# VectorE's half of the closing copy waits for TensorE only: a decode step on one NeuronCore

## The chip, the cores and the metric

The kernel runs on one core of one Trainium2 chip. The metric is the device time of one execution in microseconds (us); lower is better. The core has TensorE (PE in the profile), VectorE (DVE), ScalarE (ACT), GpSimd (POOL) and SyncE (SP), each with its own instruction stream, and 16 DMA engines. TensorE writes its results to PSUM, a small memory of 128 partitions by 8 banks (the kernel calls the whole of it `banks`); VectorE and ScalarE read PSUM and write SBUF, the main on-chip memory; DMAs move data between SBUF and HBM. The engines run side by side, and one waits for another through semaphores.

## The reference, cut to what matters

One token (batch 1, sequence 1, width 512) goes through an attention block over a cache of 16384 keys and values (32 query heads, 8 key heads of width 128), and then through a mixer with an MLP. All inputs are bfloat16.

```python
h  = x + attention(layernorm(x), k_cache, v_cache, wq, wo)
# block B, for one position:
#   its shift by one or two positions leaves only padding (zeros) when S is 1,
#   so x1 = x and w1, w2 do not count
x1 = layernorm(h)
h2 = gelu(layernorm(x1) @ w3) @ w4          # 512 -> 1792 -> 512
out = h + (x1 + h2)                          # 512 numbers
```

The result is one row of 512 bfloat16 numbers, 1 KB. The reading is 79 MB: 67 MB of keys and values and the weights `wq`, `wo`, `w3` and `w4`.

## The kernel before, in words

The keys and values come in pairs of heads, four pairs (`PAIRS`), the keys of a pair in two pieces of 4 MB; `load` puts these DMAs, and those of the weights, on SP's queue. For each pair the kernel transposes the keys on VectorE (line 583), multiplies them by the query on TensorE (line 600), takes the softmax (lines 610 to 625), multiplies by the values (line 636) and gathers the heads (lines 652 to 660). After the last pair come the product with `wo` (line 702), the second normalisation (`row_sums(1, ...)` and `variance(1)`), the product with `w3` (line 720), the gelu on ScalarE in two halves (line 729) with a transpose on VectorE behind each (line 733), and the product with `w4` (lines 737 to 751).

That last product is written to a piece of one PSUM bank, `n_ps`, in 14 steps `m`, one for each slice of `w4`. In each step four small matmuls write four groups of 32 partitions, one for each block of 128 columns of the result; every partition of a group holds the same numbers. In the middle four more matmuls (line 740) add `xsum`, which holds h plus x1. So after the last matmul the 512 numbers stand in `n_ps` as four blocks of 128 columns, on partitions 0 to 31, 32 to 63, 64 to 95 and 96 to 127.

Two copies take them out, changing float32 to bfloat16. ScalarE's (line 752) reads partitions 0 to 63 of `n_ps` into columns 0 to 127 of `fin`, an SBUF tile of 64 partitions by 256 columns. VectorE's (line 754) reads partitions 64 to 127 of the same columns of `n_ps` into columns 128 to 255 of `fin`, on the same 64 partitions. Then one DMA from SP's queue (line 755) takes rows 31 and 32 of `fin` to the output in HBM, and SP waits for its landing (line 757).

No planner sets the order: every engine runs its list of operations in the order of the program, and `Program.op` works out what each has to wait for. An operation names the tiles that it reads (`r`), those that it writes (`w`), and the PSUM banks that it touches (`bank`). It waits for the last writer of what it reads, for the writer and the readers of what it writes, and, for each bank that it names, for the last operation of every other engine that named that bank, whether that one read or wrote:

```python
for k in bank:
    for e, o in self.users.get(k, {}).items():
        if e != eng:
            need(o, False)
```

The bank of `n_ps` has the key "mn". Both copies name it, as do the matmuls of lines 740 and 747. `_wants` then turns the operations waited for into one semaphore value for each engine, and `_run` issues a wait for each value that the engine has not seen yet, ahead of the operation (line 137). A wait that doesn't fit into the operation itself stands in the trace as an instruction of its own with line 137.

On VectorE and on TensorE, `dve(None)` and `pe(None)` mark a place where a branch that is never taken is put (lines 150 and 314); VectorE's stands ahead of the copy of line 754, which is VectorE's last operation.

Of the kernel before, what the change touches and what calls it, by code (L numbers as in the profile page):

```python
# [342 lines left out]
def bass_sequential_preLN__gqa_block_cached__mixer_s_mlp__decode_kernel(  # L343
# [13 lines left out]
    with ExitStack() as ctx:  # L357
# [58 lines left out]
        fin = sb("fin", [64, 256], BF16)  # L416
# [13 lines left out]
        m_ps, n_ps = mn_ps[:, 0:256], mn_ps[:, 256:512]  # L430
# [28 lines left out]
        def dve(fn, r=(), w=(), bank=()):  # L459
            return P.op("DVE", fn, r, w, bank)  # L460
# [11 lines left out]
        def piece(cuts, m):  # L472
            return [lo <= m < hi for lo, hi in cuts].index(True)
# [23 lines left out]
        def variance(i):  # L497
# [30 lines left out]
            r=["ident", "x4"], w=["quarter"])  # L528
# [9 lines left out]
            r=["ident_f"], w=["row32"])  # L538
        dve(lambda e: e.tensor_reduce(maskdd[:, :], ident_f[:, :].rearrange("p (n d) -> p d n", d=4), AX.X, ALU.add),
            r=["ident_f"], w=["maskdd"])  # L540
# [6 lines left out]
        for z, m, key, mk in ((zo, rowgh, "zo", "rowgh"), (zd, maskgh, "zd", "maskgh")):  # L547
# [5 lines left out]
            r=["hT", (("st", 0), 0), (("st", 0), 6)] + [("v", x) for x in range(VP)], w=["xn"])  # L553
# [3 lines left out]
        for i, key in enumerate(keys):  # L557
            P.part("query", i)
            for k in range(NCH):
                pe(lambda e, k=k: e.matmul(row[:, bass.ds(P.b, 512)], copies(xn[:, k:k + 1], 128),  # L560
                                           wq_k[:, k, bass.ds(P.c, REP * DH)], start=(k == 0), stop=(k == NCH - 1)),
                   r=["xn"], also=[("v", x) for x in range(VP)], w=["n" if key == "mn" else key], bank=[key])
        P.part()
        for g in range(2):
            half = banks[64 * g:64 * g + 64, PAIRS * g:PAIRS * g + PAIRS, :].rearrange("p j c -> p (j c)")
            for b in range(2):
# [3 lines left out]
                    r=["n" if x == "mn" else x for x in keys[PAIRS * g:PAIRS * g + PAIRS]], w=["qcol"],  # L570
                    bank=keys[PAIRS * g:PAIRS * g + PAIRS])
# [120 lines left out]
        for n, (lo, hi) in enumerate(W4):  # L692
# [4 lines left out]
            r=["o_m"], w=["o_f"])  # L697
        dve(lambda e: e.tensor_copy(o_b[:, :], o_f[:, :]), r=["o_f", ("r", 0, 0)], w=["o_b"])

        for r_ in range(32):  # L700
# [3 lines left out]
               r=["o_b"] + [("r", 0, n) for n in (piece(WO, r_),) if n], w=[("O", 0)], bank=[("O", 0)])  # L704
        h_ps, hkey = banks[:, 6, :], "spare0"
        dve(lambda e: e.tensor_copy(osum[:, :], O_ps[0][:, :]), r=[("O", 0)], w=["osum"], bank=[("O", 0)])
        for q in range(4):
            pe(lambda e, q=q: e.matmul(h_ps[32 * q:32 * q + 32, 0:128], copies(row32[:, 0:1], 32),
                                       osum[:, q * 128:(q + 1) * 128], start=True, stop=True),
               r=["osum", "row32"], w=[hkey], bank=[hkey])  # L710
# [4 lines left out]
            r=["hT", (S, 0)] + [("r", 1, 0)], w=["hc"])  # L715


        for k in range(NCH):
            for q in range(4):
                pe(lambda e, k=k, q=q: e.matmul(s_ps[32 * q:32 * q + 32, 0, 0:FQ], hc[:, k, :],  # L720
                                                w3_sb[:, k, q * FQ:(q + 1) * FQ], start=(k == 0), stop=(k == NCH - 1)),
                   r=["hc"] + [("r", 1, n) for n in (piece(W3, k),) if n], w=[("s", 0)], bank=[("s", 0)])
# [3 lines left out]
            r=["hr", "xs", (S, 6)], w=["xsum"])  # L726
# [10 lines left out]
        for m in range(NHC):  # L737
            if m == NHC // 2:
                for o in range(4):
# [3 lines left out]
                       r=["ident_f", "xsum"], w=["n"], bank=["mn"])  # L743
            if m == W4[-2][0]:
                pe(None)
            for o in range(4):
# [4 lines left out]
                   r=[("hcol", 2 * m // NHC), ("r", 1, len(W3) + piece(W4, m))], w=["n"], bank=["mn"])  # L751
        act(lambda e: e.activation(fin[:, 0:128], n_ps[0:64, 0:128], ACTF.Identity),  # L752
            r=["n"], w=[("fin", 0)], bank=["mn"])
        dve(lambda e: e.tensor_copy(fin[:, 128:256], n_ps[64:128, 0:128]), r=["n"], w=[("fin", 1)], bank=["mn"])  # L754
        P.op("SP", lambda e: e.dma_start(out[0, 0:1, :].rearrange("o (q j) -> (o q) j", q=2), fin[31:33, :]),
             r=[("fin", 0), ("fin", 1)], w=["out"], dma="out")
        P.op("SP", lambda e: e.nop(), r=["out"])
# [31 lines left out]
```

## Time and profile before

| what | value |
|---|---|
| time, median of 3 runs | 190.62 us (190.58, 190.62, 190.89) |
| the profiled execution's own time | 191.29 us |
| its span, from the first to the last instruction | 189.7 us |
| mean granted TensorE clock | 0.823 |
| PE, DVE, ACT, POOL busy | 116.1, 115.4, 9.3, 5.7 us |
| read from HBM | 79.17 MB, 417 GB/s over the span |
| ScalarE's copy, line 752 | 270 ns, once |
| VectorE's copy, line 754 | 293 ns, once |

Times in the views count from the first instruction. A row of the timeline gives the start, the length, the engine, the line, the operation, and then "out<-in" with the tiles' names; in square brackets stands how long the engine was idle before it, and what ended that. The chain of waits is the work that ended last, followed back from the end: each piece has its start and length, and "issue" is time in which nothing that the profile shows was waited for. An engine's name with a q (SPq, DVEq) means its sequencer: waits and DMA issues, which are not counted as busy. The ends of matmuls are modelled.

### The profile page before, as it was taken

What the parts mean: (1) busy time and instruction counts of PE and PEld (TensorE: products, weight loads), DVE (VectorE), ACT (ScalarE), POOL (GpSimd) and SP (SyncE); (2) the same over time, 40 slices, a digit from 0 to 9 for tenths busy, and PEclk for the clock granted to TensorE, in tenths of its full rate; (3) what the DMA queues carried; (4) which work ended last, traced back from release to release, by engine and by line L of the source; (5) the groups of instructions that cost most, each with busy time, mean ns of one, the idle gap of its engine ahead of it and who ended that gap; (6) DMA issues with size and microseconds to landing.
All of it is one profiled execution on the core that took longest, in us unless ns stands there. A gap on an engine that the chain in (4) does not pass through costs nothing.

```text
span 189.7 us, 2177 instructions
## 1 busy us (share of the span) xinstructions
PE 116.1 (61%) x701; PEld 45.8 (24%) x701; DVE 115.4 (61%) x140; ACT 9.3 (5%) x16; POOL 5.7 (3%) x10
## 2 busy tenths in 40 slices
PE   1009709997194498950842999606539996094544
PEld 1004203442031143320310343202213432041113
DVE  4900799995514998945047989460469896604151
ACT  3000000000200000002000000020000000500020
POOL 1900000000000000000000000000000000000010
PEclk9999985999858589995597599975975999759955
DMA  6999999999899999997999998999999999999992
GB/s 221 442 435 442 442 442 449 442 442 442 380 435 408 435 553 428 442 442 339 435 428 422 477 401 387 442 442 435 442 442 442 428 428 415 422 402 416 411 411 106
DMA packets 3613, 79.19 MB, mean 417 GB/s; under 512 B 410, under 2 KB 540, under 8 KB 1564
## 3 DMA queue, kind: packets, MB, share of 16 engines
q1 hardware_dynamic: 3604, 79.17, 97.5%
q8 instruction: 1, 0.02, 0.0%
q10 hardware_dynamic: 8, 0.00, 0.0%
HBM read 79.17 MB, written 0.00 MB: 417 GB/s over the span
## 4 chain that ended last, share of the span: by engine, by line
DMA 66%; DVE 15%; PE 14%; issue 3%; SPq 1%; ACT 0%; DVEq 0%
DMA kb<-in_A_k_cache_dram 46%; DMA kb<-in_B_w_dram 14%; DVE kt L583 13%; PE banks L600 8%; DMA vb<-in_A_wq_dram 7%; PE banks L560 4%; SPq L434 1%; DVE qcol L567 1%; PE banks L594 1%; PE banks L747 1%; DVE qb L574 0%; PE banks L740 0%; DVE xn L551 0%; DVE fin L754 0%; ACT fin L752 0%
## 5 line engine op out<-in xcount | busy, mean ns | idle before, releaser
L583 DVE STREAM_TRANSPOSE kt<-kb 128x2048 int32<-128x2048 int32 (+1 forms) x37 | 71.3, 1988 | 5.8 <-DMA kb<-in_A_k_cache_dram 4.2
L600 PE MATMUL banks<-kt,qn 128*128 x256 | 69.8, 422 | 0.2
L600 PEld LDWEIGHTS banks<-kt,qn 128*128 x256 | 26.6, 104 | 41.9 <-issue 25.1
L636 PE MATMUL banks<-vb,pt 128*32 128x512 bf16 x256 | 22.8, 534 | 2.8 <-POOLq L449 2.8
L652 DVE TENSOR_SCALAR od<-banks,rowc 128x128 f32<-128x128 f32 x4 | 1.4, 351 | 24.7 <-PE banks L636 24.7
L594 PE MATMUL banks<-qn 128*128 128x512 bf16 x8 | 3.9, 494 | 18.4 <-DVE kt L583 18.4
L560 PE MATMUL banks<-vb,xn 128*128 x32 | 8.4, 428 | 10.1 <-DVE xn L551 10.1
L625 DVE STREAM_TRANSPOSE pt<-p_sb 64x1024 bf16<-64x1024 bf16 x8 | 9.9, 1239 | 5.4 <-ACT p_sb L621 5.3
L636 PEld LDWEIGHTS banks<-vb,pt 128*32 128x32 bf16 x256 | 8.6, 130 | 15.2 <-issue 10.3
L621 ACT ACTIVATE p_sb<-banks,bias 128x1024 bf16<-128x1024 f32 x4 | 4.5, 1114 | 155.8 <-DVE nmh L617 155.8
L643 PE MATMUL banks<-acc,zd 128*32 128x1 f32 x8 | 1.1, 203 | 17.7 <-DVE pt L625 17.7
L610 DVE TENSOR_REDUCE mx<-banks 128x1 f32<-128x1024 f32 x4 | 4.9, 1224 | 8.1 <-PE banks L600 8.1
L567 DVE STREAM_TRANSPOSE qcol<-banks 64x1024 f32<-64x1024 f32 x4 | 4.8, 1226 | 6.4 <-PE banks L560 6.4
L560 PEld LDWEIGHTS banks<-vb,xn 128*128 128x128 bf16 x32 | 3.5, 108 | 14.6 <-issue 11.8
L509 POOL TENSOR_TENSOR st<-st,expo 128x1 f32<-128x1 f32 (+1 forms) x2 | 1.3, 630 | 176.1 <-DVE st L507 176.1
L613 PE MATMUL banks<-mxd,mean 128*128 128x128 f32 x8 | 2.0, 326 | 6.6 <-DVE mxd L611 6.6
L594 PEld LDWEIGHTS banks<-qn 128*128 128x128 bf16 x8 | 0.8, 100 | 20.8 <-issue 20.5
L658 PE MATMUL banks<-od,zo 128*32 128x128 f32 x8 | 1.6, 284 | 6.5 <-DVE od L655 6.5
L643 PEld LDWEIGHTS banks<-acc,zd 128*32 128x32 f32 x8 | 0.7, 140 | 18.4 <-DVE pt L625 18.4
L655 DVE SCALAR_TENSOR_TENSOR od<-banks,rowc,od 128x128 f32<-128x128 f32 x12 | 4.2, 351 | 0.4
L702 PE MATMUL banks<-kb,o_b 128*32 128x512 bf16 x32 | 2.7, 384 | 2.4 <-DMA kb<-in_A_wo_dram 1.3
L548 DVE COPY zo<-rowgh 128x32 f32<-128x32 f32 x1 | 3.6, 3627 | 0.0
(71 smaller groups left out, 42.4 us busy)
## 6 DMA issues: line engine op xcount, KB each, us to landing
kb<-in_A_k_cache_dram SPq DMA_DIRECT2D x8, 4096.0 KB, 29.7
vb<-in_A_v_cache_dram SPq DMA_DIRECT2D x2, 4096.0 KB, 29.6
vb<-in_A_wq_dram SPq DMA_DIRECT2D x1, 4096.0 KB, 12.6
kb<-in_A_wo_dram SPq DMA_DIRECT2D x2, 1536.0 KB, 25.4
kb<-in_B_w_dram SPq DMA_DIRECT2D x2, 640.0 KB, 25.4
kb<-in_B_w_dram SPq DMA_DIRECT2D x1, 896.0 KB, 22.4
kb<-in_B_w_dram SPq DMA_DIRECT2D x2, 448.0 KB, 23.4
kb<-in_A_wo_dram SPq DMA_DIRECT2D x1, 768.0 KB, 28.5
```

What stands on the lines that cost most here:

```text
L548: dve(lambda e, z=z, m=m: e.tensor_copy(z[:, :].rearrange("p (n d) -> p n d", d=4), m[:, :, :].rearrange("p g h -> p (g h)").unsqueeze(2). ...
L560: pe(lambda e, k=k: e.matmul(row[:, bass.ds(P.b, 512)], copies(xn[:, k:k + 1], 128), wq_k[:, k, bass.ds(P.c, REP * DH)], start=(k == 0), s ...
L567: dve(lambda e, g=g, b=b, half=half: e.transpose(qcol[64 * g:64 * g + 64, 2 * b:2 * b + 2, :, :].rearrange("p e m u -> p (e m u)"), half.r ...
L583: P.op("DVE", lambda e, view=view: e.transpose(view(kt), view(kb[y])), r=[("r", y, i) for i in range(RPARTS)], w=[("kt", t + i) for i in r ...
L594: pe(lambda e: e.matmul(row[:, bass.ds(P.y, 512)], copies(none, 128), copies(none, 512), start=True, stop=False, skip_group_check=True), r ...
L600: pe(lambda e, n=n: e.matmul(row[:, bass.ds(P.y, 512)], qn[:, n, bass.ds(P.q, 128)], key_piece(P.k, n), start=False, stop=(n == 3), skip_g ...
L610: dve(lambda e: e.tensor_reduce(mx[:, :], s_all, AX.X, ALU.max), r=[("s", 0), ("s", 1)], w=["mx"], **both)
L621: act(lambda e: e.activation(p_sb[:, :], s_all, ACTF.Exp, bias=bias[:, 0:1], scale=float(SCALE), accum_out=acc[:, :]), r=[("s", 0), ("s", ...
L625: dve(lambda e, g=g: e.transpose(pt[64 * g:64 * g + 64, :, :, g, :], p_sb[64 * g:64 * g + 64, :]), r=["p"], w=["pt"])
L636: pe(lambda e, l=l, ct=ct, ch=ch: e.matmul(O_ps[0][32 * ct:32 * ct + 32, :], pt[:, l, ch, :, :].rearrange("p g u -> p (g u)"), tiles[:, l ...
L655: dve(lambda e, block=block, c=c: e.scalar_tensor_tensor(od[:, :], block, rowc[:, c:c + 1], od[:, :], ALU.mult, ALU.add), r=[key, "rowc", ...
L702: pe(lambda e, r_=r_, q=q: e.matmul(O_ps[0][32 * q:32 * q + 32, :], copies(o_b[:, r_:r_ + 1], 32), wo_sb[:, r_ * D:(r_ + 1) * D], start=(r ...
```

## The change

VectorE's copy of the second half no longer names the bank "mn". It still reads "n", which the last matmul wrote, so it still waits for TensorE. The wait for ScalarE's copy, which came only from the bank, is gone. ScalarE's copy and the closing DMA with its two inputs, `("fin", 0)` and `("fin", 1)`, are as before. No later operation names the bank.

```diff
         act(lambda e: e.activation(fin[:, 0:128], n_ps[0:64, 0:128], ACTF.Identity),
             r=["n"], w=[("fin", 0)], bank=["mn"])
-        dve(lambda e: e.tensor_copy(fin[:, 128:256], n_ps[64:128, 0:128]), r=["n"], w=[("fin", 1)], bank=["mn"])
+        dve(lambda e: e.tensor_copy(fin[:, 128:256], n_ps[64:128, 0:128]), r=["n"], w=[("fin", 1)])
         P.op("SP", lambda e: e.dma_start(out[0, 0:1, :].rearrange("o (q j) -> (o q) j", q=2), fin[31:33, :]),
              r=[("fin", 0), ("fin", 1)], w=["out"], dma="out")
```

## The prediction

> **What bounds the kernel now.** I read the page first, then the end of the chain of waits, then the timeline of the last microseconds, SP's waits, and last the DMA of that window.
>
> The page says what the run as a whole is made of:
>
> ```profile
> span 189.7 us, 2177 instructions
> PE 116.1 (61%) x701; PEld 45.8 (24%) x701; DVE 115.4 (61%) x140; ACT 9.3 (5%) x16; POOL 5.7 (3%) x10
> ...
> DMA  6999999999899999997999998999999999999992
> ...
> DMA 66%; DVE 15%; PE 14%; issue 3%; SPq 1%; ACT 0%; DVEq 0%
> ```
>
> The reader should see that the 16 DMA engines are busy in nine tenths of nearly every slice and that no engine passes 61%. The kernel is bound by its loads nearly all the way, and no edit on VectorE could shorten that stretch. But the last slice of the DMA row is a 2: at the very end the loads are over and the work hangs on the engines. The edit lies there, so the question belongs to the last slice alone. The chain of waits in the window from 187.5 us on:
>
> ```profile
> 187.42 0.34 PE banks L747 x10
> 187.76 0.02 issue
> 187.78 0.28 ACT fin L752
> 188.06 0.03 issue
> 188.09 0.02 DVEq L137
> 188.11 0.04 issue
> 188.16 0.29 DVE fin L754
> ```
>
> The last matmuls end at 187.76. ScalarE starts 0.02 us later and ends at 188.06. Only then does VectorE's wait (the row DVEq L137) go through, and its copy runs from 188.16 to 188.45. The two copies stand one behind the other, both on the chain. The timeline of the same stretch shows the same two copies, and what comes behind them:
>
> ```profile
> 187.78 0.27 ACT L752 ACTIVATE fin<-banks 64x128 bf16<-64x128 f32 x1 [3.04 <-PE banks L747]
> 188.16 0.29 DVE L754 CAST fin<-banks 64x128 bf16<-64x128 f32 x1 [2.69 <-ACT fin L752]
> 188.52 0.33 SPq L755 DMA_DIRECT2D out_dram<-fin  x1
> ```
>
> VectorE had been idle for 2.69 us when its copy began, and the profile names ScalarE's copy as what ended that. SP's waits name what the closing DMA waited for:
>
> ```profile
> SPq L137 <- DVE fin L754: 18.8, 1, 18.8
> SPq L757 <- DMA out_dram<-fin: 0.8, 1, 0.8
> ```
>
> So SP waited for VectorE's copy last, issued the output's DMA 0.07 us after it ended (188.45 to 188.52), spent 0.33 us on the issue, and waited 0.8 us more for the landing, up to the end of the span at 189.7. Nothing else goes on then. From 187.76 on, whatever ends the later of the two copies sooner ends the run sooner by as much.
>
> **The change part by part.** It removes one dependency of one instruction; nothing is moved and nothing is added.
>
> *The wait that goes.* VectorE's copy then starts when TensorE's last matmul is done. What that costs after a matmul is shown by ScalarE's row: 0.02 us of issue from 187.76 to 187.78. For VectorE itself the nearest place is its first transpose of `qcol`, which also waited for the end of matmuls:
>
> ```profile
> 14.15 8.38 PE banks L560 x32
> 22.53 0.02 issue
> 22.56 0.04 DVE qcol L567
> ```
>
> Here too it is 0.02 us of issue. I take 187.78 as the new start of VectorE's copy, the same as ScalarE's. The old start is 188.16, so the copy begins 0.38 us sooner. Put together from the chain, that is ScalarE's 0.28, then 0.03 of issue, 0.02 for the wait's own instruction, and 0.04 before the copy: 0.37, and 0.01 of rounding.
>
> *The copy itself.* It took 0.29 us alone and would now run beside ScalarE's, in the same PSUM bank but on other partitions, and both write into the same 64 partitions of `fin`. No row of the trace before has these two engines in one bank together. The bounds: the low end is nothing. The high end is that the one goes behind the other, ScalarE's whole 0.27 us. The nearest row is VectorE's pair of transposes of `hg`; the first ran while ScalarE was still writing the second half of the same tile:
>
> ```profile
> L733 DVE STREAM_TRANSPOSE hcol<-hg x2: 549/566/582, 184.4 to 184.9; 128x224 bf16<-128x224 bf16 x2
> L729 ACT ACTIVATE hg<-banks,st x2: 485/486/487, 183.9 to 184.3; 128x224 bf16<-128x224 f32 x2
> ```
>
> One of the two took 549 ns and the other 582, a difference of 0.03 us at the most that sharing can have cost there, and ScalarE's two agree within 2 ns. I take nothing for the sum, as the row that it is nearest to allows 0.03 at most, and keep 0.03 and 0.27 for the range. A gain from sharing is excluded: two copies do not shorten each other.
>
> [...]
>
> *What is late next.* VectorE's copy would end at 187.78 + 0.29 = 188.07 or 188.08; ScalarE's ends at 188.06. The two are level within 0.02 us, and the DMA waits for both. So ScalarE's copy is the next in line, and no more than 188.45 - 188.06 = 0.39 us can be had from this edit at all.
>
> *What follows.* The gap of 0.07 to the issue, the 0.33 and the 0.8 stay as they are; the DMA's issue moves from 188.52 to 188.14. The output's 1 KB has no other transfer to compete with or to be given way to, as the last loads are over: the DMA's rows for 187.3 to 188.3 list one packet, for instructions, and no data.
>
> ```profile
> DMA packets 1, 0.02 MB, mean 16 GB/s; under 512 B 0, under 2 KB 0, under 8 KB 0
> ## 3 DMA queue, kind: packets, MB, share of 16 engines
> q8 instruction: 1, 0.02, 5.8%
> ```
>
> That packet took 5.8% of 16 engines over 1.0 us, that is 0.93 us of one engine, so it lies within that window nearly whole and is over by about 188.3; the earlier output would not be carried before that, since its issue alone lasts until 188.14 + 0.33 = 188.47. I cost it at nothing.
>
> *The sum.* 0.38 us off. The profiled execution's 191.29 (its span of 189.7 and 1.6 around it) would become 190.91. That execution stands 0.67 above the median of the unprofiled runs, 190.62; the piece saved is made of ScalarE's copy and semaphore steps, which should be the same there. So 190.62 - 0.38 = 190.24 us.
>
> The size matters for the chances: 0.2% of 190.62 is 0.38 us, about what a measurement of this kernel can tell from no change. The whole gain stands just on that border. Against the mean of the three runs, 190.70, the forecast is 0.24% down.
>
> **The rivals.**
>
> *The two copies give way to each other.* If one engine holds the bank, or the write side of `fin`, until it is through, VectorE starts its part at 187.78 + 0.27 = 188.05 at the earliest and ends at 188.34, 0.11 us before the old end: 190.62 - 0.11 = 190.51. For it speaks that the overlap is new in this kernel. Against it speak the transposes above, which lost 0.03 at most beside ScalarE, and that each copy has its own partitions.
>
> *The edit doesn't reach the clock.* The wait could still be there by another way, through SP's wait for both halves for one, and the time stays at 190.62. That wait exists, but ScalarE's half is done at 188.06, ahead of everything else in the sum, so it can hide no more than 0.02 us. What is left is that something unseen ends the run, and the chain ends with VectorE's copy and the DMA with no gap unaccounted for.
>
> *The code of the copy is not there yet: slower.* VectorE's stream becomes one instruction shorter, as the wait of its own goes, and the copy takes its place. If the copy fell into a block of instructions that is only loaded when it is called for, the load would come after 187.78. The profile has the price of a small transfer from issue to landing, 0.33 + 0.8 = 1.1 us for the output. The copy would start at 188.9 in place of 188.16, 0.74 later: 191.36. It decides from a start later than 188.16 + 0.38 = 188.54 on; anything earlier than 188.16 still leaves a gain. For it speaks that there is an instruction packet in just this window, and that 2.69 us of waiting could have hidden it until now. Against it: the wait's instruction ran 0.03 after ScalarE's end, and the copy 0.04 after that, at 188.16, while the packet of 0.93 us that lies after 187.3 can hardly have been over before 188.23. So neither needed that packet, and the copy now stands where the wait stood.
>
> [...]
>
> **How the numbers follow.** The forecast, both copies beside each other, has 0.78: it needs only what the chain shows. The rival of giving way has 0.07, no change 0.05, the late code 0.10. Within the forecast the gain lies between 0.35 (with the 0.03 of the transposes) and 0.39 (the most that ScalarE leaves), and the runs before scatter from 190.58 to 190.89, most of it upward. I put 0.52 of the 0.78 on the far side of 0.2%, since the mean before lies higher than the median, and 0.26 on the near side. Faster is then 0.52; within 0.2% is 0.26 + 0.07 + 0.05 = 0.38; slower is 0.10.
>
> The range: its low end is the most that can be had, 190.23, less 0.18, a little over half of the scatter of 0.31 between the runs before: 190.05. Its high end takes in the giving way (190.51) and no change (190.62) with a little scatter: 190.70. Left out are the late code and the tails.
>
> **What the profile of the changed kernel would show.** The row of DVEq L137 ahead of the copy gone; both copies starting at the same time, 0.02 us after the last matmul; VectorE's idle time before its copy ended by the matmuls of line 747, and 0.38 us shorter, about 2.3; its length still 0.29 and ScalarE's 0.27; the issue of the output 0.38 sooner relative to the last matmul, and the 0.33 and 0.8 behind it the same. Lengths of 0.3 to 0.56 would show the giving way. A start of the copy well after the last matmul, with "issue" ahead of it, would show late code. The prediction is wrong if the start of the copy stays tied to ScalarE, if the last matmul itself comes at another time by more than 0.2 us, or if the landing of the output grows by what was saved.

## The result, and the profile after

| what | before | after |
|---|---|---|
| median of 20 runs, us | 190.88 (190.58 to 191.33) | 190.51 (190.36 to 190.93) |
| ratio after to before | | 0.9982, 95% interval 0.9976 to 0.9988 |
| the profiled execution's own time, us | 191.29 | 190.56 |
| its span, us | 189.7 | 189.0 |

The kernel is faster by 0.18%, between 0.12% and 0.24%: 0.34 us by the ratio, 0.37 us by the medians. The forecast was a gain of 0.38 us. The time itself, 190.51, lies in the range and 0.27 us over the forecast of 190.24, because with 20 runs the kernel before stands at 190.88 and not at the 190.62 of the three runs that the forecast was made from.

The end of the chain of waits after the change (start, length, what):

```profile
186.59 0.81 PE banks L747 x28
187.40 0.02 issue
187.43 0.29 DVE fin L754
```

ScalarE's copy and the row DVEq L137 are gone from it: VectorE's copy follows the last matmul directly, with 0.02 us of issue. The timeline shows where ScalarE's copy went:

```profile
186.38 1.00 PE L747 MATMUL banks<-kb,hcol 128*32 128x128 bf16 x28
187.43 0.27 ACT L752 ACTIVATE fin<-banks 64x128 bf16<-64x128 f32 x1 [2.63 <-PE banks L747]
187.43 0.29 DVE L754 CAST fin<-banks 64x128 bf16<-64x128 f32 x1 [1.92 <-PE banks L747]
187.79 0.33 SPq L755 DMA_DIRECT2D out_dram<-fin  x1
```

Both copies start at 187.43, and each names the matmuls of line 747 as what ended its idle time. The DMA goes out at 187.79, 0.36 us behind the start of the first copy; before it was 188.52 - 187.78 = 0.74. The difference, 0.38, is the sum's term. The rows of the tile `fin` show the lengths to the nanosecond, and SP's waits show the rest of the way:

```profile
L752 ACT ACTIVATE fin<-banks x1: 272/272/272, 187.4 to 187.4; 64x128 bf16<-64x128 f32 x1
L754 DVE CAST fin<-banks x1: 293/293/293, 187.4 to 187.4; 64x128 bf16<-64x128 f32 x1
```
```profile
SPq L137 <- DVE fin L754: 18.5, 1, 18.5
SPq L757 <- DMA out_dram<-fin: 0.8, 1, 0.8
```

Side by side, the copies take 272 and 293 ns, against 270 and 293 one behind the other. The issue of the output and its landing are as they were.

A trap lies in the two spans. They differ by 0.7 us, twice the gain. The rest is not the edit's: before the change, the profiled execution had its last matmul end at 187.76, and after it at 187.40, both ahead of the first line that was changed. The timeline of before, a few rows ahead of the copies, shows what held it up:

```profile
186.16 0.41 PE L747 MATMUL banks<-kb,hcol 128*32 128x128 bf16 x8 [0.38 <-DMA kb<-in_B_w_dram]
```

In that execution the matmuls waited 0.38 us for a late piece of the last weights, and its own time, 191.29, lies 0.41 over the median of the kernel before. By the chains of waits that piece landed at 186.11 there, and at 185.83 in the experiment with a long shared read below, whose matmuls waited 0.39 us for it too; its transfer had begun later by nearly as much, at 160.12 against 159.87. Two of the experiments keep one copy behind the other, as before the change, and their last matmuls end at 187.47 and 187.35: when the last matmul ends does not hang on the edit. A gain at the end has to be read from the last matmul on, not from the span.

### The profile page after: what moved, and what is told of

It is laid out like the page before. It is cut to its first block, busy times and chain, and to the rows that moved or that the text cites. A ratio compares the mean times of both kernels' runs of the same rounds, so it can differ in the third digit from the quotient of the medians.

```text
span 189.0 us, 2176 instructions
## 1 busy us (share of the span) xinstructions
PE 116.6 (62%) x701; PEld 45.4 (24%) x701; DVE 115.3 (61%) x140; ACT 9.3 (5%) x16; POOL 5.7 (3%) x10
## 4 chain that ended last, share of the span: by engine, by line
DMA 53%; PE 26%; DVE 15%; issue 3%; ACT 1%; SPq 0%; DVEq 0%; ACTq 0%
DMA kb<-in_A_k_cache_dram 31%; DMA kb<-in_A_wo_dram 15%; PE banks L600 13%; DVE kt L583 10%; DMA vb<-in_A_wq_dram 6%; PE banks L560 5%; PE banks L636 3%; DVE pt L625 1%; PE banks L747 1%; PE banks L720 1%; PE banks L594 1%; PE banks L702 1%; DVE qcol L567 1%; DVE mx L610 1%; ACT p_sb L621 1%
## 5 line engine op out<-in xcount | busy, mean ns | idle before, releaser
L600 PE MATMUL banks<-kt,qn 128*128 x256 | 68.4, 411 | 0.4
L600 PEld LDWEIGHTS banks<-kt,qn 128*128 x256 | 26.0, 102 | 41.3 <-issue 25.3
L560 PE MATMUL banks<-vb,xn 128*128 x32 | 9.2, 460 | 9.7 <-DVE xn L551 9.7
L702 PE MATMUL banks<-kb,o_b 128*32 128x512 bf16 x32 | 3.6, 532 | 2.5 <-DMA kb<-in_A_wo_dram 1.5
L706 DVE COPY osum<-banks 128x512 f32<-128x512 f32 x1 | 0.7, 693 | 5.1 <-PE banks L702 5.1
```

The source lines that it names most:

```text
L600: pe(lambda e, n=n: e.matmul(row[:, bass.ds(P.y, 512)], qn[:, n, bass.ds(P.q, 128)], key_piece(P.k, n), start=False, stop=(n == 3), skip_g ...
L702: pe(lambda e, r_=r_, q=q: e.matmul(O_ps[0][32 * q:32 * q + 32, :], copies(o_b[:, r_:r_ + 1], 32), wo_sb[:, r_ * D:(r_ + 1) * D], start=(r ...
```

## The experiments

Eight kernels were run. All edits are against the changed kernel unless said otherwise. One measure serves for all of them: the time from the start of the first closing copy to the issue of the output's DMA, from the timeline. It leaves out how late the loads were.

| kernel | first copy starts | output issued | apart | median, us | ratio to before |
|---|---|---|---|---|---|
| before | 187.78 | 188.52 | 0.74 | 190.88 | 1 |
| after | 187.43 | 187.79 | 0.36 | 190.51 | 0.9982 (0.9976 to 0.9988) |
| a wait that is long over | 187.50 | 187.86 | 0.36 | 190.55 | 0.9988 (0.9979 to 0.9997) |
| VectorE first, ScalarE waits | 187.50 | 188.18 | 0.68 | 190.79 | 0.9997 (0.9988 to 1.0006) |
| before, one more copy | 187.37 | 188.27 | 0.90 | 191.04 | 1.0010 (1.0001 to 1.0019) |
| after, one more copy | 187.48 | 187.84 | 0.36 | 190.47 | 0.9977 (0.9968 to 0.9986) |
| ScalarE alone | 187.55 | 187.85 | 0.30 | 190.88 | 1.0004 (0.9995 to 1.0013) |
| VectorE alone | 187.49 | 187.81 | 0.32 | 190.97 | 1.0005 (0.9996 to 1.0014) |
| a long read shared | 187.52 | 187.89 | 0.37 | 190.65, one run | not timed |
| SP's waits in the other order | 187.37 | 187.71 | 0.34 | 190.47 | 0.9981 (0.9972 to 0.9990) |

The kernel before stood at 190.85 beside the runs of the first four experiments and at 190.84 beside the others.

**Is it ScalarE's copy, or is it the wait as such?** The change also takes away an instruction. Here a wait is put in its place, for a no-op of GpSimd that is over long before.

```diff
+        P.op("POOL", lambda e: e.nop(), r=[(S, 7)], w=["tick"])
         dve(None)
...
-        dve(lambda e: e.tensor_copy(fin[:, 128:256], n_ps[64:128, 0:128]), r=["n"], w=[("fin", 1)])
+        dve(lambda e: e.tensor_copy(fin[:, 128:256], n_ps[64:128, 0:128]), r=["n", "tick"], w=[("fin", 1)])
```

> The changed kernel, but VectorE's copy waits for a no-op of GpSimd as well, which is done about 4 us earlier. So VectorE has as many waits to go through as before the change, and its code is as long, but ScalarE's copy is not among them. Serial theory (the gain came from no longer standing behind ScalarE): the copies start within 0.03 us of each other and the time is that of the changed kernel, 0.34 us under before (0.25 to 0.45). Rival, the gain came from the wait's own instruction or from the code being one instruction shorter: the copy starts some 0.1 us or more after ScalarE's and a third or more of the gain is lost, or all of it, time 0 to 0.25 us under before.

```profile
187.50 0.27 ACT L753 ACTIVATE fin<-banks 64x128 bf16<-64x128 f32 x1 [3.00 <-PE banks L748]
187.50 0.29 DVE L755 CAST fin<-banks 64x128 bf16<-64x128 f32 x1 [2.29 <-PE banks L748]
187.86 0.33 SPq L756 DMA_DIRECT2D out_dram<-fin  x1
```

Both copies start at 187.50, and the distance to the DMA is 0.36, as in the changed kernel. By the medians it is 0.30 us faster than before; the ratio gives 0.23 us, with 0.06 to 0.40 in its interval, which by itself would fit the rival as well; the copies' start decides. So this wait, for something that was long over, cost nothing (0.36 us in both kernels), and the instruction that it adds to VectorE's code played no part. What the edit removed is the standing behind ScalarE.

This wait did not stand right ahead of the copy, however. VectorE's sequencer went through it 2.8 us earlier:

```profile
L137 DVEq EVENT_SEMAPHORE  x1: 21/21/21, 184.7 to 184.7; - x1
```

So the run does not show what a wait with an instruction of its own costs when it is the last to come. The chain of the changed kernel has a place where VectorE waits for ScalarE without such an instruction, at the first transpose of `hg`:

```profile
183.94 0.50 ACT hg L729
184.44 0.02 issue
184.46 0.59 DVE hcol L733
```

The step from ScalarE to VectorE takes 0.02 us there, and 0.10 (188.06 to 188.16) in the kernel before, where the wait was an instruction of its own. By these two rows an estimated 0.08 of the 0.38 us was the price of that form of wait, and 0.30 the standing behind the copy. A kernel that keeps the wait but puts it into the copy itself was not run.

**Does the order matter?** This is the kernel before with its two copies exchanged, so that ScalarE waits for VectorE.

```diff
+        dve(lambda e: e.tensor_copy(fin[:, 128:256], n_ps[64:128, 0:128]), r=["n"], w=[("fin", 1)], bank=["mn"])
         act(lambda e: e.activation(fin[:, 0:128], n_ps[0:64, 0:128], ACTF.Identity),
             r=["n"], w=[("fin", 0)], bank=["mn"])
-        dve(lambda e: e.tensor_copy(fin[:, 128:256], n_ps[64:128, 0:128]), r=["n"], w=[("fin", 1)])
```

> The kernel before, with the two copies in the other order: VectorE first, ScalarE waits for it. Serial theory: one copy stands behind the other again; ScalarE starts 0.29 + 0.08 = 0.37 us after VectorE, the same gap as before the change the other way round, and ends 0.64 us after the matmuls instead of 0.67; time within 0.1 us of before. Rival, that it was something particular to VectorE's wait behind ScalarE (a slow wait, late code): ScalarE's copy follows with a smaller gap and the time falls by 0.1 to 0.3 us.

The end of its chain of waits:

```profile
187.47 0.02 issue
187.50 0.30 DVE fin L752
187.80 0.02 issue
187.82 0.02 ACTq L137
187.84 0.04 issue
187.88 0.27 ACT fin L753
```

Again one copy stands behind the other, and ScalarE starts 0.38 us after VectorE, where 0.37 was expected. The time is that of before within its interval. A small thing was not expected: the DMA goes out 0.03 us after ScalarE's end (188.15 to 188.18), where it was 0.07 after VectorE's in the kernel before. The last experiment follows that up.

**Does the end follow the length of ScalarE's work?** A second copy by ScalarE, of the same half into a spare tile that nobody reads, is put between the two copies, once in the kernel before and once in the changed one.

```diff
+        spare = sb("spare", [64, 128], BF16)
...
             r=["n"], w=[("fin", 0)], bank=["mn"])
+        act(lambda e: e.activation(spare[:, :], n_ps[0:64, 0:128], ACTF.Identity),
+            r=["n"], w=["spare"], bank=["mn"])
```

In the kernel before:

> The kernel before, with a second ScalarE copy of the same half into a spare tile that nobody reads, between the two copies; VectorE waits for it, as it names the same bank. Serial theory: VectorE starts one ScalarE copy later, 0.25 to 0.30 us, and the time is 0.25 to 0.30 us over before. Rival, that the end hangs on something else (the landing of the last weights, the output's transfer): time as before, within 0.1 us.

In the changed kernel:

> The changed kernel with the same second ScalarE copy. Serial theory: VectorE doesn't wait for it, SP doesn't either, so the time is that of the changed kernel, 0.34 us under before (0.25 to 0.45), and 0.6 us under the kernel before with the same extra copy. Rival, the two engines give way to each other in the bank: VectorE's copy gets longer than 0.293 us, now that ScalarE reads beside it all the while, and the gain is smaller by as much.

The chain of the first, and the timeline of the second:

```profile
187.37 0.27 ACT fin L753
187.64 0.17 ACT spare L755
187.81 0.03 issue
187.84 0.02 DVEq L137
187.86 0.04 issue
187.90 0.29 DVE fin L757
```
```profile
187.48 0.27 ACT L753 ACTIVATE fin<-banks 64x128 bf16<-64x128 f32 x1 [2.60 <-PE banks L748]
187.48 0.29 DVE L757 CAST fin<-banks 64x128 bf16<-64x128 f32 x1 [1.89 <-PE banks L748]
187.65 0.26 ACT L755 ACTIVATE spare<-banks 64x128 bf16<-64x128 f32 x1
187.84 0.33 SPq L758 DMA_DIRECT2D out_dram<-fin  x1
```

In the kernel before, VectorE is pushed back by the added copy, and the end with it: 0.90 in place of 0.74, and 0.19 us of time by the medians. In the changed kernel the same copy costs nothing (190.47), and the two differ by 0.57 us. So the end follows ScalarE's length as long as the bank is named, and not when it isn't. The expectation of 0.25 to 0.30 was too high: the second copy adds 0.17 us to the chain, though it is 0.26 long, as it begins 0.17 us after the first while that one still runs. Behind the first copy the second one's price was 0.17 us here, not its length. VectorE's copy, now with ScalarE reading the bank beside it from start to end, takes 0.29 us as before.

**Is sharing a bank free, or was 128 columns too short to see it?** In the middle of the last part VectorE copies the attention's sum, 128 partitions by 512 columns, out of one bank. It is split here by partitions, and neither half names the bank.

```diff
-        dve(lambda e: e.tensor_copy(osum[:, :], O_ps[0][:, :]), r=[("O", 0)], w=["osum"], bank=[("O", 0)])
+        dve(lambda e: e.tensor_copy(osum[0:64, :], O_ps[0][0:64, :]), r=[("O", 0)], w=[("osum", 0)])
+        act(lambda e: e.activation(osum[64:128, :], O_ps[0][64:128, :], ACTF.Identity), r=[("O", 0)], w=[("osum", 1)])
...
-               r=["osum", "row32"], w=[hkey], bank=[hkey])
+               r=[("osum", 0), ("osum", 1), "row32"], w=[hkey], bank=[hkey])
```

> The changed kernel, and in the middle of the last part the copy of the attention's sum, which VectorE did alone (0.69 us, 128 partitions by 512 columns), is split by partitions: VectorE takes 0 to 63, ScalarE 64 to 127, out of the same bank at the same time. Sharing is free: VectorE's half still takes 0.69 us, within 0.01, and ScalarE's some 0.6 with no start later than VectorE's. Giving way: VectorE's half gets longer by 0.05 us or more, up to twice as long.

The rows of the two halves, and then VectorE's row for the undivided copy in the kernel before:

```profile
L707 ACT ACTIVATE osum<-banks x1: 592/592/592, 178.7 to 178.7; 64x512 f32<-64x512 f32 x1
```
```profile
L706 DVE COPY osum<-banks x1: 682/682/682, 178.7 to 178.7; 64x512 f32<-64x512 f32 x1
```
```profile
L706 DVE COPY osum<-banks x1: 692/692/692, 178.9 to 178.9; 128x512 f32<-128x512 f32 x1
```

VectorE's half, with ScalarE reading the same bank beside it for 592 ns, takes 682 ns; alone, over all partitions, it took 692. VectorE gives nothing away. Its half alone was not run, nor ScalarE's, but the next experiment has VectorE's copy of 128 partitions at 0.29 us, as long as that of 64. This is one execution, and an effect of a twentieth would be 35 ns. What happens on the same partitions was not tried.

**Can one copy do for both?** In the rows above, the length of VectorE's copies goes by the columns and hardly by the partitions: 682 ns for 64 partitions by 512 columns, 692 for 128 by 512, 293 for 64 by 128. If the closing copies do the same, one engine can take all 128 partitions in the time of 64, and SP waits once. (`BLOCK` says which block of columns goes to which group of 32 partitions.)

```diff
-BLOCK = (0, 2, 1, 3)
+BLOCK = (0, 1, 2, 3)
...
-        fin = sb("fin", [64, 256], BF16)
+        fin = sb("fin", [128, 128], BF16)
...
+        act(lambda e: e.activation(fin[:, :], n_ps[:, 0:128], ACTF.Identity), r=["n"], w=["fin"], bank=["mn"])
+        P.op("SP", lambda e: e.dma_start(out[0, 0:1, :].rearrange("o (q j) -> (o q) j", q=4), fin[0:128:32, :]),
+             r=["fin"], w=["out"], dma="out")
```

The other kernel has `dve(lambda e: e.tensor_copy(fin[:, :], n_ps[:, 0:128]), ...)` in place of ScalarE's line.

> The changed kernel with one copy in place of two: ScalarE takes all 128 partitions of the product into a tile of 128 by 128, and the output's DMA takes four rows of 256 bytes from partitions 0, 32, 64 and 96 in place of two rows of 512 (the blocks of w4 come in plain order for that). Theory (a copy's length goes by its columns, and SP has one wait in place of two): the copy takes 0.27 us as before, SP issues the DMA 0.02 us after its end in place of 0.06, and the last matmul and the issue lie 0.29 to 0.30 us apart in place of 0.37; time 0.05 to 0.08 us under the changed kernel, 0.42 us under before. Rival, four short rows from four partitions cost more than two: the issue (0.33) or the landing (0.8) gets longer by 0.1 us or more and the time is that of the changed kernel or over it.

> The same with VectorE's copy alone, 0.29 us for all 128 partitions. Theory: 0.02 us later than with ScalarE alone, the last matmul and the issue 0.33 us apart; time 0.04 us under the changed kernel, 0.38 us under before. Rival as for ScalarE alone.

The timeline of the kernel with ScalarE alone, and its waits on SP:

```profile
187.55 0.28 ACT L752 ACTIVATE fin<-banks 128x128 bf16<-128x128 f32 x1 [2.60 <-PE banks L747]
187.85 0.62 SPq L753 DMA_DIRECT2D out_dram<-fin  x1
```
```profile
SPq L753 <- ACT fin L752: 18.4, 1, 18.4
SPq L755 <- DMA out_dram<-fin: 1.0, 1, 1.0
```

The first half of the theory holds: the copy takes 0.28 us for twice the partitions, and the DMA goes out 0.30 us after the copy's start in place of 0.36 (0.32 with VectorE alone). The gain is lost behind that, as the rival had it and by more: the issue takes 0.62 us in place of 0.33, and the wait for the landing is 1.0 in place of 0.8. Both kernels end level with before, where the theory had them under the changed kernel. Whether the number of rows, their 256 bytes or the step of 32 partitions makes the issue long was not taken apart.

**The gap ahead of the output.** SP's two waits are named in the other order, so that VectorE's, the later one, goes with the DMA itself.

```diff
-             r=[("fin", 0), ("fin", 1)], w=["out"], dma="out")
+             r=[("fin", 1), ("fin", 0)], w=["out"], dma="out")
```

> The changed kernel, with the two inputs of the output's DMA named in the other order, so that SP waits for ScalarE's copy with an instruction of its own and for VectorE's, the later one, with the DMA itself. Theory (a wait's own instruction that comes last costs what lies between it and the DMA, 0.05 us): the issue comes 0.02 to 0.04 us after VectorE's end in place of 0.06; time 0.02 to 0.05 us under the changed kernel, which the times will hardly show and the profile's rows will. Rival: the gap of 0.06 is SP's own and stays.

```profile
187.37 0.27 ACT L752 ACTIVATE fin<-banks 64x128 bf16<-64x128 f32 x1 [2.61 <-PE banks L747]
187.37 0.29 DVE L754 CAST fin<-banks 64x128 bf16<-64x128 f32 x1 [1.89 <-PE banks L747]
187.71 0.33 SPq L755 DMA_DIRECT2D out_dram<-fin  x1
```

The DMA goes out 0.34 us after the copies' start in place of 0.36, 0.05 after VectorE's end (187.66) in place of 0.07. The order of the waits matters by 0.02 us here. A gap of 0.02 to 0.04 was expected, so 0.05 is a miss. SP's waits show that the one with an instruction of its own is now for ScalarE's copy:

```profile
SPq L137 <- ACT fin L752: 18.5, 1, 18.5
```

That copy ends at 187.64, only 0.02 us ahead of VectorE's. In the changed kernel the DMA went out 0.07 us after the end of the copy that the separate wait was for (187.72 to 187.79); 0.07 behind 187.64 is 187.71, the measured issue. By this estimate the separate wait was still the last step. The median of 190.47 and the ratio of 0.9981 can't tell it from the changed kernel; no version that was run is clearly faster than that one.

## Why the prediction was right, point by point

*The bound.* Only the stretch behind the last matmul counted, and in it the chain from matmul to copy to copy to DMA. The trace after shows the same chain with one copy less.

*The wait that goes, 0.38 us.* Right in place and size: 0.74 became 0.36 from the first copy's start to the DMA's issue, in one execution each, and the medians fell by 0.37. The start of VectorE's copy at the same moment as ScalarE's, 0.02 us behind the last matmul, is there to the hundredth. That VectorE's tie to ScalarE cost the time, and not the number of its instructions, is shown by the wait that is long over (0.36) and by the added copy, which costs time in the kernel before and none in the changed one. The sum's terms behind ScalarE's end, 0.03 + 0.02 + 0.04, belong to the tie as well; most of them come from the wait being an instruction of its own, by the estimate above.

*The copy itself, nothing.* Right: 293 ns beside ScalarE as alone, and 682 ns against 692 for a read four times as long. The 0.03 us kept from the transposes as the near bound was not needed.

*What is late next.* Right: the copies end at 187.70 and 187.72, level within 0.02, and VectorE's is still the later one.

*What follows.* Right: issue 0.33, landing 0.8, the gap to the issue 0.07.

*The rivals.* Giving way fell with the two shared reads, and only with them: its time was put at 190.51, which is the measured median. The two times agree by luck, since the rival was counted down from the low level of the three runs. That each copy has its own partitions, which the prediction put against this rival, was the author's argument: no run has the copies read the same partitions, so none shows whether it counts. No change fell with the result. The late code fell with the result too. The DMA's rows of the changed kernel for 186.6 to 187.6 show that the packet of instructions was on its way while the copies ran:

```profile
DMA  0000000000000009000000000000000000000000
...
q8 instruction: 1, 0.02, 7.1%
```

It starts in the sixteenth of 40 slices, at 186.98 at the earliest, and takes 7.1% of 16 engines over 1.0 us, 1.14 us of one engine, so by this estimate it is under way until about 188.1. Both copies started at 187.43, 0.02 us behind the matmul. Neither needed that packet; which engine's instructions it carried, the trace does not say. That code is loaded only when it is called for, as this rival supposes, no run shows.

*How the numbers follow.* Here two things were off. The level: the forecast took the median of three runs, 190.62, and 20 runs gave 190.88. The range of 190.05 to 190.70 held the time only because it had been kept wide towards the top, for rivals that did not happen. That is luck: the gain was forecast for the right reason, the time was not. And the chances: 0.52 stood on a gain of over 0.2% for the reason that the mean of the runs before lay above their median. That was no reason, as a higher level before raises the time after as well and leaves the gain of 0.38 where it is. The measured gain, 0.18% with 0.12 to 0.24% around it, lies on the near side of the border and does not settle the far side; it is clear of zero.

*The signs that missed.* VectorE's idle time was forecast at about 2.3 us and was 1.92. That was worked out with the late matmul of the one profiled execution before; with the last matmul 0.36 us earlier, the idle time is shorter by about as much. The same matmul set off a sign of being wrong: the prediction was to be wrong if the last matmul came at another time by more than 0.2 us, and it came 0.36 earlier. The sign was badly chosen, since it compares single executions: the two kernels that keep one copy behind the other had that matmul end at 187.47 and 187.35, as early as the changed one with 187.40.

## What to carry to other kernels

Look at the last microsecond of a kernel that is bound by its loads: in this kernel nothing hid work there, and a dependency between two engines that share a bank but neither data nor partitions cost a whole copy and three semaphore steps, 0.37 us. Where a dependency tracker keeps engines apart by bank, look for such waits in the chain and ask what each protects; on separate halves of the partitions the two closing copies took as long together as one behind the other, within 2 ns. For readers of the same partitions nothing here shows that the wait can go. And measure such a gain from the last event that the edit can't have touched, since the span of a single execution moved by as much again for other reasons.

## What the runs showed that was not expected

- A wait of VectorE for ScalarE, last to come and with an instruction of its own, took 0.10 us from ScalarE's end to VectorE's start; in the operation itself it took 0.02.
- A second ScalarE copy of 64 by 128 behind the first one adds 0.17 us to the chain, not its 0.26.
- An output of four rows of 256 bytes, from partitions 32 apart, has an issue of 0.62 us and 1.0 us of waiting for the landing, against 0.33 and 0.8 for two rows of 512 bytes from neighbouring partitions: 0.5 us for the same 1 KB.
- The order in which SP's waits are named moves the output by 0.02 us, and with ScalarE's copy last and its wait on the DMA itself the gap ahead of the issue was 0.03 us in place of 0.07.
